# An attention, MoE and bilinear kernel: the order of its first stage as a written-out list, scale constants in four steps, a second key buffer

## The chip, the cores and the metric

The kernel runs on one core of a Trainium2 chip. The metric is the device time of one execution in microseconds (us). The engines are TensorE (PE; PEld is its weight load), VectorE (DVE), ScalarE (ACT), GpSimd (POOL) and SyncE (SP, whose queue issues most DMAs). L with a number is a line of the kernel before.

## The reference

Causal attention with a forget bias, then a mixture of eight experts whose gate is normalised eight times over rows and columns, then a bilinear layer:

```
cum = np.cumsum(np.maximum(s, 0.0), axis=-1)
bias = -(cum[:, :, :, None] - cum[:, :, None, :])
scores = np.where(causal, -1e9, scale * q @ k.T + np.minimum(bias, 0.0))
x = softmax(scores) @ v
P = exp(x @ w_gate - max), eight times divided by row and column sums
out += P[:, e:e + 1] * (np.maximum(x @ w1[e], 0.0) @ w2[e])      for e in 0..7
result = ((out @ w_a) * (out @ w_b)) @ w_out
```

There are 2 batches, 8 heads, 576 tokens each and a head size of 64; the model width is 512, an expert's inner width 1024, the bilinear layer's 1536. All in fp32.

## The kernel before, in words

**Number form.** Most products are made of fp16 pairs: a value is scaled by a power of two and split into a high part (hi, L367 or L372) and a low part, the scaled value less the high one (lo, L382 on VectorE, L376 and L377 on GpSimd). A product is three fp16 matmuls. For each scale the largest value of a tensor is bounded first: by a square with a running sum on ScalarE (`sumsq`, L365, or L602 for the weights), whose squares themselves are not used, or by an absolute maximum on VectorE (`absmax`, L362).

**Attention.** The 1152 tokens are nine tiles of 128; tile 8 holds the two tails of 64. Tiles 0 and 4 open a batch and are done in fp32 (`first_tile`, L1149 to L1220: the maximum L1197, the subtraction L1198, the exponential L1201, transposes L1205 copied by L1208, the product with v L1213, the division L1228 to L1233). The other tiles use the fp16 pairs. For them `k_prep` (L790) makes two forms of each key tile, `kn2` (hi, and beside it the forget bias as three fp16 parts, `caug`) and `kn1` (hi and lo), and `q_prep` (L816) likewise makes `qa` (hi with `qaug`) and `qb`. Each is turned by a DMA transpose on SP's queue, into `ka2` and `ka1` for the keys (L810) and `b` for the queries (L828, L834). Tiles 1 to 3 then take the row maximum (`row_max`, L843, matmuls L856, reductions L860), a shift of it (`shift`, L895) and probabilities (`probs`, L919: exponentials L960 and L972, low parts L974 or L975). Tiles 5 to 8 go by `row_path` (L1012), whose probabilities are turned by DMA transposes (L1039).

**Scale constants.** `scales` (L700) makes for each batch, from the squares of k and q, the scales SK and SQ, the forget bias' scale AL, the product CF and the rest, in a tile `cst` of one column each: `consts` (L728 to L737) and `consts2` (L739 to L755), tiny VectorE instructions. `augs` (L765) makes from AL and CF the forget parts `caug` and `qaug` on GpSimd.

**Expert 0.** As each attention tile comes out (`x_tile`, L1220; its transposes L1244, copies L1249 and L1251, or casts L1254, L1256 with a DMA transpose L1257), expert 0's first product runs for it in quarters (`h_quad`, L1330, matmuls L1343 to L1345) and then its second (`y_part`, L1354, L1363 to L1365). The gate's logits follow (L1292 to L1301). Once all nine tiles are through, experts 1 to 7 run with seven products for eight (`h_seven`, L1736) and then the bilinear layer. Expert 1's weights w1[1] are loaded and split (`w_prep`, L579) before that, in eight pieces of 256 KB.

**What sets the order.** Nothing is issued directly. A `Graph` (L59) records each operation with its engines, a planner's cost and what it reads and writes; `emit` (L235) ranks the operations, moves groups of them by a table `GROUPS`, places them in time by `schedule` (L103), choosing an engine where several are allowed, and issues them in that order. It does so for all operations up to `cut` (attention, expert 0, w1[1]) and then for the rest. An engine runs its instructions strictly in the issued order.

```
        for o in self.ops[:self.cut]:
            o[4] -= o[10]
        self.pool = 1.0
        state = self.schedule(0, self.cut)
```

**Buffers.** `junk` (one tile) takes the squares of k, q and v. `kn1` and `kn2` are one buffer each; `qa` has two, `qb` one.

## Time and profile before

| | |
|---|---|
| median of three runs | 1024.3 us (1023.85 to 1025.38) |
| the profiled execution, first to last instruction | 1023.8 us, 0.5 below the median |
| TensorE busy | 995.2 us, 97% |
| VectorE busy | 777.5 us, 76% |
| ScalarE busy | 547.8 us, 54% |
| GpSimd busy | 103.7 us, 10% |
| chain that ended last | PE 88%, DVE 5%, DMA 4%, ACT, issue and POOL 1% each |

The chain is followed back from the last instruction to what released each step. Shares of the whole hide that the program has two parts: attention with expert 0 up to about 209 us, and dense products after. The windows and timelines below are read for the first part; "idle before" in square brackets names what released an instruction.

### The profile page before, as it was taken

How to read it: one execution, taken by the hardware profiler on the slowest of the kernel's cores; microseconds unless marked ns; L12 is line 12 of the kernel's file. 1: busy time of each engine (PE TensorE's matmuls, PEld its weight loads, DVE VectorE, ACT ScalarE, POOL GpSimd, SP SyncE). 2: the span in 40 equal slices, each digit the busy share in tenths (PEclk: the TensorE clock that was granted, in tenths of full speed). 3: DMA queues.
4: the chain of work that ended last, by engine and by line, in shares of the span. 5: the costliest groups of instructions: out<-in, count | busy, mean ns of one | idle time of the engine just before them, and what ended most of it. 6: DMA issues, size and time to landing. Idle time of an engine off the chain costs nothing.

```text
span 1023.8 us, 18873 instructions
## 1 busy us (share of the span) xinstructions
PE 995.2 (97%) x7514; PEld 630.9 (62%) x7514; DVE 777.5 (76%) x1642; ACT 547.8 (54%) x1029; POOL 103.7 (10%) x163
## 2 busy tenths in 40 slices
PE   6879999999999999999999999999999999999998
PEld 3667776756447646745754774575476464555777
DVE  7789788299957998994899898489988895667402
ACT  7868876375246637734663772565364454545220
POOL 2447616000000000000000000000000000000000
PEclk7689999999999999999999999999999999999999
DMA  9886999222024244114325412422545532313202
GB/s 251 195 144 121 178 161 148 49 83 84 1 89 142 99 179 170 64 47 160 124 83 206 165 42 82 167 82 83 206 165 203 137 83 83 125 42 124 83 25 69
DMA packets 151976, 121.34 MB, mean 119 GB/s; under 512 B 113344, under 2 KB 127680, under 8 KB 147280
## 3 DMA queue, kind: packets, MB, share of 16 engines
...
q8 instruction: 59, 0.97, 0.4%
...
## 4 chain that ended last, share of the span: by engine, by line
PE 88%; DVE 5%; DMA 4%; ACT 1%; issue 1%; POOL 1%; SPq 0%; DVEq 0%; POOLq 0%; ACTq 0%
PE yb L1364 11%; PE yb L1365 11%; PE yb L1363 11%; PE yb L1757 4%; PE yb L1756 4%; PE yb L1755 4%; PE mb L1755 3%; PE mb L1757 3%; PE mb L1756 3%; PE yb L1985 2%; PE yb L1986 2%; PE yb L1987 2%; PE mb L1320 2%; PE mb L1322 2%; PE mb L1321 2%; PE mb L1986 2%
## 5 line engine op out<-in xcount | busy, mean ns | idle before, releaser
L1363 PE MATMUL yb<-wun,ht 128*128 128x512 f16 x504 | 191.0, 379 | 0.0
L1364 PE MATMUL yb<-wun,ht 128*128 128x512 f16 x504 | 191.0, 379 | 0.0
L1365 PE MATMUL yb<-wun,ht 128*128 128x512 f16 x504 | 191.0, 379 | 0.0
L1365 PEld LDWEIGHTS <-ht 128*128 128x128 f16 x504 | 49.3, 98 | 59.4
L1363 PEld LDWEIGHTS <-ht 128*128 128x128 f16 x504 | 49.4, 98 | 58.8
L1364 PEld LDWEIGHTS <-ht 128*128 128x128 f16 x504 | 49.3, 98 | 58.8
L382 DVE SCALAR_TENSOR_TENSOR wun<-stage,sc,wun 128x1024 f16<-128x1024 f32 (+1 forms) x70 | 77.1, 1126 | 8.6 <-ACT wun L368 8.2
L1755 PE MATMUL yb<-sx,wun 128*128 128x288 f16 x288 | 82.4, 286 | 0.0
L1756 PE MATMUL yb<-sx,wun 128*128 128x288 f16 x288 | 82.4, 286 | 0.0
L1757 PE MATMUL yb<-sx,wun 128*128 128x288 f16 x288 | 82.4, 286 | 0.0
L1815 DVE SCALAR_TENSOR_TENSOR acc<-yb,pe,acc 128x512 f32<-128x512 f32 x63 | 47.3, 750 | 41.8 <-PE yb L1365 40.6
L1756 PEld LDWEIGHTS <-wun 128*128 128x128 f16 x672 | 65.7, 98 | 17.8 <-issue 0.7
L1755 PEld LDWEIGHTS <-wun 128*128 128x128 f16 x672 | 65.7, 98 | 17.1
L1757 PEld LDWEIGHTS <-wun 128*128 128x128 f16 x672 | 65.8, 98 | 16.6
L365 ACT ACTIVATE jk<-stage 128x1024 f16<-128x1024 f32 x52 | 54.8, 1054 | 33.6 <-DMA stage<-in_moe_w_dram 33.0
L368 ACT ACTIVATE wun<-stage,sc 128x1024 f16<-128x1024 f32 (+1 forms) x62 | 61.9, 1034 | 19.3 <-PE yb L1365 14.7
L368 ACT ACTIVATE wun<-h,sc 128x1024 f16<-128x1024 f32 x36 | 41.2, 1145 | 27.2 <-issue 23.9
L1755 PE MATMUL mb<-xt,wun 128*128 128x288 f16 x192 | 54.9, 286 | 0.3 <-ACT yb L1774 0.3
L1757 PE MATMUL mb<-xt,wun 128*128 128x288 f16 x192 | 54.9, 286 | 0.0
L1756 PE MATMUL mb<-xt,wun 128*128 128x288 f16 x192 | 54.9, 286 | 0.0
L1344 PE MATMUL mb<-xt,wun 128*128 128x128 f16 x288 | 53.4, 226 | 1.0 <-DVE xt L1251 1.0
L1343 PE MATMUL mb<-xt,wun 128*128 128x128 f16 x288 | 53.5, 226 | 0.3 <-DVE logit L1300 0.3
...
## 6 DMA issues: line engine op xcount, KB each, us to landing
...
```

What stands on the lines that cost most here:

```text
L365: nc.scalar.activation(out, src, AF.Square, accum_out=dst)
L368: nc.scalar.activation(hi, src, AF.Copy, scale=scale)
L382: eng.scalar_tensor_tensor(out=lo, in0=src, scalar=scale, in1=hi, op0=ALU.mult, op1=ALU.subtract)
L1343: nc.tensor.matmul(p, lhsT=wh, rhs=xh, start=(c == 0), stop=False)
L1344: nc.tensor.matmul(p, lhsT=wh, rhs=xl, start=False, stop=False)
L1363: nc.tensor.matmul(pp, lhsT=hh, rhs=wh, start=(f == 0), stop=False)
L1364: nc.tensor.matmul(pp, lhsT=hh, rhs=wl, start=False, stop=False)
L1365: nc.tensor.matmul(pp, lhsT=hl, rhs=wh, start=False, stop=(f == KF - 1))
L1755: nc.tensor.matmul(p, lhsT=wh, rhs=xh, start=first and ch == 0, stop=False, skip_group_check=True)
L1756: nc.tensor.matmul(p, lhsT=wh, rhs=xl, start=False, stop=False, skip_group_check=True)
L1757: nc.tensor.matmul(p, lhsT=wl, rhs=xh, start=False, stop=ch == 1, skip_group_check=True)
L1815: g.add("DVE", 663, lambda t=t, z=z: nc.vector.scalar_tensor_tensor(out=acc[:, t], in0=yb[z], scalar=pe[:, t, e:e + 1], in1=acc[:, t], op0 ...
```

## The change

- The order and the engine choice of every operation up to `cut` are read from a list, `ORDER` (a number is 4 times the operation plus the choice); the ranking, the random seeds and `GROUPS` are gone. The operations after `cut` are placed by the same rules as before.
- Squares of k, q, v and the first tiles' v go to parts of `ka1` and `ka2` that are not yet filled (`spare`), each its own, instead of `junk`.
- The constants are made in four operations: `consts` (SK, SQ), `alpha_` (AL), `factors` (CF), `consts2` (the rest). Forget parts depend on AL or CF alone.
- `caug` may be made on VectorE in four instructions (before: six on GpSimd), `qaug` on either engine.
- `kn2` becomes two buffers `kn[0][0]` and `kn[0][1]` used in turn; `kn1` becomes `kn[1][0]`, still one. The forget half lies first in `kn` and `qa`, so `ut` has 16 columns and needs no memset. `sel` is multiplied only for the first batch's keys.
- `ntail` lies in `xt`, `sc` has 476 columns.

```diff
-        self.stale = True
-        for seed in SEEDS:
-            self.rerank(seed)
-        for o in self.ops[:self.cut]:
-            o[4] -= o[10]
-        self.pool = 1.0
-        state = self.schedule(0, self.cut)
+        state = self.schedule(0, self.cut, None, ORDER)
...
+    def spare(a, i, t):
+        return (ka1, ka2)[a][:, 4 * i:4 * i + 4, t * 128:(t + 1) * 128], ("ka", ("kn1", "kn2")[a], t)
...
-                g.add("ACT", 700, lambda r=r, c=c, t=t, src=src: (
-                    sumsq(mxs[r, c:c + 1], src[t][r], junk[r])),
-                      r=[mk] + (keys[t] if t < 2 * NJ else [keys[t][b]]), w=[mk + (x, j)], rank=rank)
+                jk, jkk = spare(1 - x, 0 if t < 2 * NJ else b, t)
+                g.add("ACT", 700, lambda r=r, c=c, t=t, src=src, jk=jk: (
+                    sumsq(mxs[r, c:c + 1], src[t][r].rearrange("p (a d) -> p a d", a=4), jk[r])),
+                      r=[mk] + (keys[t] if t < 2 * NJ else [keys[t][b]]), w=[mk + (x, j), jkk], rank=rank)
...
-            nc.vector.tensor_scalar(bits(a), bits(a), EXPM, None, op0=ALU.bitwise_and)
-            nc.vector.tensor_scalar(c[:, IK:IK + 2], a, 2.0 ** -6 * h, None, op0=ALU.mult)
-
-        def consts2():
+
+        def alpha_():
             c = cst[:, b]
             col = lambda i: c[:, i:i + 1]
+            a = t4[:, 0:2]
+            nc.vector.tensor_scalar(bits(a), bits(a), EXPM, None, op0=ALU.bitwise_and)
+            nc.vector.tensor_scalar(c[:, IK:IK + 2], a, 2.0 ** -6 * 2.0 ** 63, None, op0=ALU.mult)
             nc.vector.tensor_scalar(col(ESC), col(IK), col(IQ), qk_scale, op0=ALU.mult, op1=ALU.mult)
             nc.vector.tensor_scalar(col(TA), col(ESC), 2.0 ** 17 / qk_scale, bank[:, 130:131], op0=ALU.mult, op1=ALU.add)
             nc.vector.tensor_scalar(bits(col(TB)), bits(col(TA)), EXPM, EXPM, op0=ALU.bitwise_and, op1=ALU.bitwise_xor)
             nc.vector.tensor_scalar(col(AL), col(TB), 2.0 ** 12, None, op0=ALU.mult)
+
+        def factors():
+            c = cst[:, b]
+            col = lambda i: c[:, i:i + 1]
             nc.vector.tensor_scalar(bits(col(TA)), bits(col(TA)), EXPM, None, op0=ALU.bitwise_and)
             nc.vector.tensor_scalar(col(IAL), col(TA), 2.0 ** -13 / qk_scale, None, op0=ALU.mult)
             nc.vector.tensor_scalar(col(CF), col(SK), col(SQ), col(IAL), op0=ALU.mult, op1=ALU.mult)
+
+        def consts2():
+            c = cst[:, b]
+            col = lambda i: c[:, i:i + 1]
             nc.vector.tensor_scalar(col(NAF), col(ESC), col(AL), -1.0, op0=ALU.mult, op1=ALU.mult)
             nc.vector.tensor_scalar(col(APL), col(AL), 14.0 * math.log(2.0), None, op0=ALU.mult)
...
-        g.add("DVE", 930, consts, r=zk, w=[("sk", b)], rank=rank)
-        g.add("DVE", 2050, consts2, r=zk + [("sk", b)], w=[("cst", b)], rank=rank)
+        g.add("DVE", 640, consts, r=zk, w=[("sk", b)], rank=rank)
+        g.add("DVE", 990, alpha_, r=zk + [("sk", b)], w=[("al", b)], rank=rank)
+        g.add("DVE", 490, factors, r=[("al", b)], w=[("cf", b)], rank=rank)
+        g.add("DVE", 950, consts2, r=[("cf", b)], w=[("cst", b)], rank=rank)
...
-            cm = ctmp[:, ts]
+            nc.vector.tensor_scalar(caug[:, ts, :, 0], cumc[:, ts], cc(ci, AL), None, op0=ALU.mult)
+            nc.vector.scalar_tensor_tensor(out=cm, in0=cumc[:, ts], scalar=cc(ci, AL), in1=caug[:, ts, :, 0], op0=ALU.mult, op1=ALU.subtract)
+            nc.vector.tensor_copy(caug[:, ts, :, 1], cm)
+            nc.vector.tensor_tensor(out=caug[:, ts, :, 2], in0=cm, in1=caug[:, ts, :, 1], op=ALU.subtract)
+
+        def fp():
             nc.gpsimd.tensor_scalar(cm, cumc[:, ts], cc(ci, AL), 1.0, op0=ALU.mult, op1=ALU.mult)
             nc.gpsimd.tensor_copy(caug[:, ts, :, 0], cm)
             for x in (1, 2):
                 nc.gpsimd.tensor_tensor(out=cm, in0=cm, in1=caug[:, ts, :, x - 1], op=ALU.subtract)
                 nc.gpsimd.tensor_copy(caug[:, ts, :, x], cm)
...
+        def f2(e):
             o = ones[:, 0:H * 3].rearrange("p (h a) -> p h a", h=H)
-            nc.gpsimd.tensor_scalar(qaug[:, ci], o, cc(ci, CF), 1.0, op0=ALU.mult, op1=ALU.mult)
...
-        ck = [("cst", b) for b in ((ci,) if ci < 2 else (0, 1))]
-        g.add("POOL", 1600, f, r=["cumc"] + ck, w=[("caug", ci)], rank=rank)
-        g.add("POOL", 280, f2, r=["ones"] + ck, w=[("qaug", ci)], rank=rank)
+            e.tensor_scalar(qaug[:, ci], o, cc(ci, CF), 1.0, op0=ALU.mult, op1=ALU.mult)
+
+        ck = [("cst", b) for b in (0, 1)]
+        g.add(("DVE", "POOL"), (561, 1600), (f, fp), r=["cumc"] + ([("al", ci)] if ci < 2 else ck), w=[("caug", ci), "ctmp"], rank=rank)
+        g.add(("POOL", "DVE"), (280, 110), (lambda: f2(nc.gpsimd), lambda: f2(nc.vector)), r=["ones"] + ([("cf", ci)] if ci < 2 else ck), w=[("qaug", ci)], rank=rank)
...
-        hi = lambda: kn2[:, :, 0]
+        z = kc_[0] % NKN
+        kc_[0] += 1
+        hi = lambda: kn[0][z][:, :, 1]
...
-        g.add(("ACT", "POOL"), (713, 690), hi_any(hi, src, cc(ci, SK)), r=krk[t] + kk, w=[("kn2", 0)], rank=rank)
-        g.add(("DVE", "POOL"), (763, 1900), lo_any(lambda: kn1[:, :, 1], src, cc(ci, SK), hi), r=kk + [("kn2", 0)], w=krk[t] + [("kn1", 1)], rank=rank)
...
+        g.add(("ACT", "POOL"), (713, 690), hi_any(hi, src, cc(ci, SK)), r=krk[t] + kk, w=[("kn", z, 1)], rank=rank)
+        g.add(("DVE", "POOL"), (763, 1900), lo_any(lambda: kn[1][0][:, :, 1], src, cc(ci, SK), hi), r=kk + [("kn", z, 1)], w=krk[t] + [("kn", 0, 2)], rank=rank)
...
+        for x, dst, nm in ((0, ka2, "kn2"), (1, ka1, "kn1")):
...
-                g.add("-", 3000, lambda: None, r=[("kn2", 0), ("kn2", 1)], w=behind)
-            g.add("SP", 1600, lambda dst=dst, src_=src_: nc.sync.dma_start_transpose(
-                out=dst[:, :, t * 128:(t + 1) * 128], in_=src_.rearrange("p h a d -> p (h a d)")),
-                r=[(nm, 0), (nm, 1)] + behind, w=[("ka", nm, t)], rank=rank - 5, issue=1300.0)
+                g.add("-", 3000, lambda: None, r=[("kn", z, 0), ("kn", z, 1)], w=behind)
+            g.add("SP", 1600, lambda dst=dst, x=x: nc.sync.dma_start_transpose(
+                out=dst[:, :, t * 128:(t + 1) * 128], in_=kn[x][z * (1 - x)].rearrange("p h a d -> p h (a d)")),
+                r=[("kn", 0, 2 + y) if x else ("kn", z, y) for y in range(2)] + behind, w=[("ka", nm, t)], rank=rank - 5, issue=1300.0)
...
+ORDER = (
+    0, 80, 148, 4, 28, 96, 36, 8, 156, 92, 104, 100, 16, 84, 88, 108, 24, 884, 1632, 12, 76, 888, 20, 160,
+    44, 48, 172, 40, 192, 189, 320, 304, 164, 180, 300, 328, 152, 176, 52, 184, 316, 56, 208, 112, 204, 325, 484, 332,
...
-SEEDS = (0, 0, 0, 0)
+NKN = 2
```

The list moves instructions as follows.

ScalarE at the start, about 17 to 24 us in the profile (p: the two halves of tile 0's probabilities, pt: their transposes, wun: w1[0]'s high parts, acc and raw: k and q). Before:

```order
L1201 ACTIVATE p_0_105<-p_0_105 128x512
L365 ACTIVATE junk,sc<-acc 128x512
L368 ACTIVATE wun_75<-stage_73,sc 128x512 x2
L368 ACTIVATE wun_76<-stage_74,sc 128x512 x2
L1201 ACTIVATE p_1_106<-p_1_106 128x512
L365 ACTIVATE junk,sc<-acc 128x512 x3
L365 ACTIVATE junk,sc<-raw 64x512
L1208 ACTIVATE pt_107<-st_138 128x512
L1208 ACTIVATE pt_108<-st_139 128x512
```
Now:

```order
L1148 ACTIVATE p_0_106<-p_0_106 128x512
L1148 ACTIVATE p_1_107<-p_1_107 128x512
L1155 ACTIVATE pt_108<-st_137 128x512
L294 ACTIVATE wun_75<-stage_73,sc 128x512
L579 DMA vs_95<-in_v_dram 128x8x64
L1155 ACTIVATE pt_109<-st_138 128x512
L291 ACTIVATE ka_93,sc<-acc 128x4x128
L294 ACTIVATE wun_76<-stage_74,sc 128x512 x2
L291 ACTIVATE ka_92,sc<-acc 128x4x128
```
Both exponentials and the first copy of the transposes now stand ahead of all high parts and squares; one high part and a DMA issue stand between the two copies.

VectorE at the first batch's constants (cst; L742 to L745 make AL, L746 to L748 CF, the rest up to L755 what later tiles need; mb and h: expert 0), before, about 43 to 46 us in the profile:

```order
L744 TENSOR_SCALAR cst<-cst 128x1
L745 TENSOR_SCALAR cst<-cst 128x1
L746 TENSOR_SCALAR cst<-cst 128x1
L747 TENSOR_SCALAR cst<-cst 128x1
L748 TENSOR_SCALAR cst<-cst 128x1
L749 TENSOR_SCALAR cst<-cst 128x1
L750 TENSOR_SCALAR cst<-cst 128x1
L751 SCALAR_TENSOR_TENSOR cst<-cst 128x1
L752 TENSOR_SCALAR cst<-cst 128x1
L753 MEMSET cst 128x1
L755 COPY cst<-cst 64x14
L1350 SCALAR_TENSOR_TENSOR h_0_79<-mb_84,h_0_79 128x512
```
Now (L665 to L670 are `alpha_`, L675 to L677 `factors`, L706 opens the forget parts):

```order
L667 TENSOR_SCALAR cst<-cst 128x1
L668 TENSOR_SCALAR cst<-cst,xp_139 128x1
L669 TENSOR_SCALAR cst<-cst 128x1
L670 TENSOR_SCALAR cst<-cst 128x1
L308 SCALAR_TENSOR_TENSOR qb<-acc,cst,qa_100 128x8x64
L675 TENSOR_SCALAR cst<-cst 128x1
L676 TENSOR_SCALAR cst<-cst 128x1
L677 TENSOR_SCALAR cst<-cst 128x1
L308 SCALAR_TENSOR_TENSOR wun_77<-stage_73,sc,wun_77 128x512
L496 TENSOR_REDUCE sc<-xp_140 1x1
L1297 SCALAR_TENSOR_TENSOR h_0_79<-mb_84,h_0_79 128x512
L706 TENSOR_SCALAR caug<-cumc,cst 128x32
```
A low part of q and three other instructions stand between the steps, the six of `consts2` have moved past both row maxima of tile 4 (L1144), and the forget parts, six instructions of GpSimd before, follow here as four (L706 to L709).

GpSimd in the stretch of tiles 1 to 3, about 65 to 85 us in the profile (vs: v's high and low parts; pt: low parts of probabilities). Before:

```order
L975 TENSOR_TENSOR pt_111<-p_0_105,pt_111 128x512
L975 TENSOR_TENSOR pt_107<-p_1_106,pt_107 128x512
L975 TENSOR_TENSOR pt_108<-p_0_105,pt_108 128x512
L514 MEMSET vs_95 128x40x2
L516 MEMSET vs_95 64x4x2 x2
L975 TENSOR_TENSOR pt_109<-p_1_106,pt_109 128x512
L1254 CAST xhl<-xb 128x512
L1256 TENSOR_TENSOR xhl<-xb,xhl 128x512
L372 TENSOR_SCALAR kn_97<-raw,cst 128x8x64
L975 TENSOR_TENSOR pt_110<-p_0_105,pt_110 128x512
```
Now:

```order
L298 TENSOR_SCALAR vs_94<-vs_95,sc 128x8x64
L917 CAST pt_110<-p_1_107 128x512
L298 TENSOR_SCALAR vs_94<-vs_95,sc 128x8x64
L302 TENSOR_SCALAR vs_95<-vs_95,sc 128x512
L303 TENSOR_TENSOR vs_94<-vs_95,vs_94 128x8x64
L921 TENSOR_TENSOR pt_110<-p_1_107,pt_110 128x512
L917 CAST pt_111<-p_0_106 128x512
L921 TENSOR_TENSOR pt_111<-p_0_106,pt_111 128x512
L302 TENSOR_SCALAR vs_95<-vs_95,sc 128x512
L303 TENSOR_TENSOR vs_94<-vs_95,vs_94 128x8x64
```
Two high parts and, of the five low parts of v that VectorE made here before, four (each L302 with L303; the third and fourth follow behind these rows) now stand on GpSimd.

SP's queue: before, every load of q, k and v but three of k stands ahead of the first transpose, which is one of kn. Now six loads of v, three of k and one of q, for the second batch, stand among the first fifteen transposes, and the first two transposes are of qb and qa, the third and fourth of the two kn buffers. The number of transposes is the same, 68. Of the eight loads of w1[1], before six in this queue between transposes near 92 to 103 us and two from ScalarE's queue, two stay between transposes here, four stand at the end around the last transpose of xt, and two are issued from ScalarE's queue.

## Rows read from the trace of the kernel before

**Rows 1.** Windows, two stretches: us, then busy of PE, PEld, DVE, ACT, POOL, clock, DMA share, GB/s.
```profile
63.00:103.00 40.00, 34.73 (x529) 28.59 (x528) 37.52 (x94) 32.82 (x57) 26.50 (x43) 1.00 0.74 130
...
209.00:1024.00 815.00, 810.58 (x5170) 493.92 (x5168) 620.58 (x1235) 398.51 (x733) 16.40 (x31) 1.00 0.32 110
```

**Rows 2.** Windows again, three stretches cut where the granted clock changes.
```profile
12.00:42.70 30.70, 22.22 (x125) 17.22 (x126) 22.26 (x67) 25.76 (x68) 7.99 (x10) 0.50 1.01 236
42.70:56.40 13.70, 11.28 (x100) 7.19 (x98) 11.53 (x39) 11.73 (x30) 8.49 (x17) 1.00 0.78 161
56.40:63.20 6.80, 6.41 (x31) 5.94 (x32) 4.91 (x20) 1.96 (x4) 2.60 (x4) 0.50 0.64 129
```

**Rows 3.** Timeline, VectorE, 15 to 33 us: start, us, engine, line, operation, names, idle before.
```profile
17.13 0.68 DVE L1198 TENSOR_TENSOR p<-ss,mxr 128x512 f32<-128x512 f32 x1
...
27.89 0.69 DVE L362 TENSOR_REDUCE sc<-stage 128x1 f32<-128x512 f32 x1 [1.26 <-DMA stage<-in_moe_w_dram]
```

**Rows 4.** Timeline, ScalarE, 15 to 32 us.
```profile
17.24 2.56 ACT L368 ACTIVATE wun<-stage,sc 128x512 f16<-128x512 f32 x4
19.71 0.61 ACT L1201 ACTIVATE p<-p 128x512 f32<-128x512 f32 x1
20.23 0.61 ACT L365 ACTIVATE junk<-acc 128x512 f16<-128x512 f32 x1
...
22.47 0.63 ACT L365 ACTIVATE junk<-raw 64x512 f16<-64x512 f32 x1
...
23.10 1.06 ACT L1208 ACTIVATE pt<-st 128x512 f32<-128x512 f32 x2
...
30.96 0.63 ACT L602 ACTIVATE wun<-stage 128x512 f16<-128x512 f32 x1 [0.27 <-DMA stage<-in_moe_w_dram]
...
31.59 0.58 ACT L1249 ACTIVATE xt<-st 128x512 f16<-128x512 f32 x1
```

**Rows 5.** Timeline, TensorE, 19 to 34 us and 60 to 63 us.
```profile
23.73 3.68 PE L1213 MATMUL xp<-vf,pt 128*128 128x65 f32 x16 [2.07 <-ACT pt L1208]
...
32.95 0.27 PE L1344 MATMUL mb<-xt,wun 128*128 128x128 f16 x1 [0.40 <-DVE xt L1251]
...
60.88 0.40 PE L856 MATMUL ss<-ka,b 128*128 128x256 f16 x1
```

**Rows 6.** Timeline, VectorE, 33 to 50 us.
```profile
38.95 1.40 DVE L382 SCALAR_TENSOR_TENSOR wun<-stage,sc,wun 128x512 f16<-128x512 f32 x2
...
40.89 0.15 DVE L732 TENSOR_SCALAR sc<-xp 128x2 f32<-128x2 f32 x1
...
41.92 1.05 DVE L382 SCALAR_TENSOR_TENSOR wun<-stage,sc,wun 128x512 f16<-128x512 f32 x1
...
44.90 0.37 DVE L755 COPY cst<-cst 64x14 f32<-64x14 f32 x1
```

**Rows 7.** Timeline, GpSimd (POOL), 33 to 60 us.
```profile
45.58 1.48 POOL L771 TENSOR_SCALAR ctmp<-cumc,cst 128x32 f32<-128x32 f32 x1
...
49.16 0.29 POOL L779 TENSOR_SCALAR qaug<-ones,cst 128x24 f16<-128x24 f32 x1
```

**Rows 8.** Timeline, SyncE queue, 45 to 64 us.
```profile
49.64 1.36 SPq L810 DMA_TRANSPOSE ka<-kn  x1
```

**Rows 9.** Waits, GpSimd 40 to 63 us, ScalarE 50 to 63 us: total, times, longest.
```profile
POOL kn L803 <- DMA ka<-kn: 2.1, 1, 2.1
...
ACT kn L368 <- DVE kn L382: 2.5, 1, 2.5
```

**Rows 10.** Lines, VectorE and GpSimd, 63 to 103 us: count, busy us, mean ns, idle before.
```profile
L382 DVE SCALAR_TENSOR_TENSOR vs<-vs,sc,vs 128x512 f16<-128x512 f32 x5 | 5.5, 1108 | 0.0
...
L377 POOL TENSOR_TENSOR qb<-raw,qa 128x512 f16<-128x512 f32 x1 | 1.5, 1545 | 0.1
```

**Rows 11.** Timeline, SyncE queue, 90 to 106 us.
```profile
99.33 3.86 SPq L594 DMA_DIRECT2D stage<-in_moe_w_dram  x4
```

**Rows 12.** Timeline, ScalarE, 183 to 210 us.
```profile
195.56 0.63 ACT L602 ACTIVATE wun<-stage 128x512 f16<-128x512 f32 x1 [2.96 <-DMA xt<-xhl]
```

More of the change, by code (lines that the diff above doesn't have):

```diff
@@ L90, in add @@
             fn = tuple((lambda q=q: fn0(q)) for fn0 in (fn,) for q in self.queues)
-        self.ops.append([eng, cost, fn, sorted(deps), rank, issue, rel, load, rows, 0.0, *GROUPS.get(self.at, (0.0, 0.0)), self.at])
+        self.ops.append([eng, cost, fn, sorted(deps), rank, issue, rel, load, rows, self.at])
     def begin(self):
@@ L101, in begin, with schedule @@
         self.costs = [o[1] if isinstance(o[1], tuple) else (o[1],) for o in self.ops]
-    def schedule(self, first=0, last=None, state=None):
+    def schedule(self, first=0, last=None, state=None, given=None):
         ops, succ, engs, costs = self.ops, self.succ, self.engs, self.costs
@@ L113, in schedule @@
         order = []
+        for x in given or ():
+            order.append(divmod(x, 4))
+        given, order = order, []
         while pend:
             per = {}
-            for i in pend:
+            for i in [given[len(order)][0]] if given else pend:
                 es, cs, rd = engs[i], costs[i], ready[i]
@@ L119, in schedule @@
                 room = dma - BACKLOG if ops[i][7] else 0.0
-                if len(es) > 1:
+                if given:
+                    k = given[len(order)][1]
+                elif len(es) > 1:
                     pen = PENQ if ops[i][7] else PEN
-                    k = min(range(len(es)), key=lambda k: max(free[es[k]], rd[es[k]], room) + cs[k] + (self.pool * ops[i][11] if es[k] == "POOL" else pen.get(es[k], 0.0)))
+                    k = min(range(len(es)), key=lambda k: max(free[es[k]], rd[es[k]], room) + cs[k] + pen.get(es[k], 0.0))
                 e = es[k]
@@ L297, in forgetting_attention_moe_bilinear_kernel @@
     clampf = clampi.bitcast(F32)
-    sc = const.tile([128, 480], F32, name="sc")
+    sc = const.tile([128, 476], F32, name="sc")
     isx = const.tile([128, NTL], F32, name="isx")
@@ L395, in forgetting_attention_moe_bilinear_kernel @@
     vs = [ap.tile([128, NBLK, H, 130], F16, name=f"vs{b}") for b in range(B)]
-    kn1 = ap.tile([128, H, 2, D], F16, name="kn1")
-    kn2 = ap.tile([128, H, 2, D], F16, name="kn2")
+    kn = [[ap.tile([128, H, 2, D], F16, name=f"kn{x}{i}") for i in range((NKN, 1)[x])] for x in range(2)]
     qa = [ap.tile([128, H, 2, D], F16, name=f"qa{i}") for i in range(2)]
@@ L412, in forgetting_attention_moe_bilinear_kernel @@
     sel = ap.tile([128, H, 2 * H], F32, name="sel")
-    ut = [ap.tile([128, 128], F16, name=f"ut{i}") for i in range(2)]
+    ut = [ap.tile([128, 2 * H], F16, name=f"ut{i}") for i in range(2)]
     cst = ap.tile([128, 3, 16], F32, name="cst")
@@ L423, in forgetting_attention_moe_bilinear_kernel @@
     vf = ap.tile([128, H, 65], F32, name="vf")
-    ntail = ap.tile([H, 128], F32, name="ntail")
     nid = ap.tile([H, H], F32, name="nid")
@@ L508, in forgetting_attention_moe_bilinear_kernel @@
     g.at = "cum"
-    for x, key in ((kn2, ("kn2", 1)), (qa[0], ("qa", 0, 1)), (qa[1], ("qa", 1, 1))):
-        g.add("POOL", 500, lambda x=x: nc.gpsimd.memset(x[:, :, 1], 0.0), w=[key], rank=0.5)
+    for x, key in (*((kn[0][i], ("kn", i, 0)) for i in range(NKN)), (qa[0], ("qa", 0, 0)), (qa[1], ("qa", 1, 0))):
+        g.add("POOL", 500, lambda x=x: nc.gpsimd.memset(x[:, :, 0], 0.0), w=[key], rank=0.5)
     def vone(b):
@@ L528, in forgetting_attention_moe_bilinear_kernel @@
     g.add("POOL", 600, consts_, w=["sel"], rank=0.6)
-    for z in range(2):
-        g.add("POOL", 200, lambda z=z: nc.gpsimd.memset(ut[z], 0.0), w=[("ut", z)], rank=0.7)
     wkey = {}
@@ new lines, in k_prep @@
+        g.add(("DVE", "POOL", "ACT"), (320, 690, 620), (lambda: nc.vector.tensor_copy(kn[1][0][:, :, 0], hi()), lambda: nc.gpsimd.tensor_copy(kn[1][0][:, :, 0], hi()),
+              lambda: nc.scalar.activation(kn[1][0][:, :, 0], hi(), AF.Copy)), r=[("kn", z, 1)], w=[("kn", 0, 3)], rank=rank)
+        if ci != kci[z]:
+            kci[z] = ci
+            if ci < 2 and any(x not in ROWP for x in range(max(ci * NJ, 1), (ci + 1) * NJ) if x not in FIRST):
+                g.add(("POOL", "DVE"), (400, 230), tuple(lambda e=e: e.tensor_scalar(kn[0][z][:, :, 0, 0:2 * H], sel, cc(ci, CF), 1.0, op0=ALU.mult, op1=ALU.mult) for e in (nc.gpsimd, nc.vector)),
+                      r=["sel"] + [("cf", b) for b in bs], w=[("kn", z, 0)], rank=rank)
```

134 lines of the change are left out of this document (28 added, 106 removed), and 65 rows, old and new, of tables (GROUPS, ORDER).

## The prediction

> **What bounds the kernel now.** I read the windows first, because the shares of the whole mix two programs. From 209 us to the end TensorE is busy 810.6 of 815 us at full clock [rows 1]: experts 1 to 7 and the bilinear layer leave 4.4 us of idle time, and the change does not touch their operations. Whatever it does to the time it does before 209 us. There TensorE does 995.2 - 810.6 = 184.6 us of work (table and rows 1), so at most 24 us of idle time are to be had, and some more where the clock is low: the granted clock is 0.50 (1.2 GHz) from 12 to 42.7 us and once more from 56.4 to 63.2 us, and 1.00 (2.4 GHz) between and after [rows 2].
>
> The timelines then say who holds TensorE up. Until 33 us it waits for tile 0, which passes from VectorE to ScalarE and back. From 33 to 61 us it has expert 0 of tile 0 and tile 4's fp32 work, while the constants, the forget parts and the first transposes are made; the first row maximum starts at 60.88 us [rows 5]. From 63 to 103 us VectorE bounds: busy 37.52 of 40 us, TensorE 34.73 [rows 1].
>
> **The change part by part.**
>
> *A, the start.* Tile 0's second subtraction ends at 17.13 + 0.68 = 17.81 [rows 3], but its exponential starts at 19.71, behind four high parts of w1[0] [rows 4]: 1.9 us. Then four squares (first 20.23, last 22.47) stand ahead of the copies of the transposes at 23.10 [rows 4], and the product with v had waited 2.07 us when it started at 23.73 [rows 5]; the first of two copies takes half of 1.06, so 1.5 us were the squares'. That product ends at 27.41; VectorE's division for it comes only behind an absolute maximum that waited 1.26 us for its DMA and ran from 27.89 to 28.58 [rows 3]: 0.9 us allowing 0.25 for the hand-over, an estimate. The copy into xt at 31.59 stands behind a square begun at 30.96 that also waited for its DMA [rows 4]: 0.6 us. All four stand the other way round now: 1.9 + 1.5 + 0.9 + 0.6 = 4.9 us, less one high part of 2.56 / 4 = 0.64 that now stands between the two copies: expert 0 starts about 4.3 us sooner than at 32.95 [rows 5]. I pass on none of it by itself. The row maximum at 60.88 does not wait for expert 0, so TensorE would only stand idle later instead. Bounds: 0 and -4.3.
>
> *B, constants in steps.* Before, the scales are out at 41.5, the last constant ends at 44.90 + 0.37 = 45.27, GpSimd begins the forget parts at 45.58 and ends them and qaug at 49.16 + 0.29 = 49.45, and the first transpose is issued at 49.64 [rows 6, 7, 8]. Now one low part of w2 instead of two stands ahead of L732 (0.70 less, from 1.40 for two [rows 6]); then AL takes six instructions of about 0.2, a low part of q 0.7 to 1.05, CF three of 0.2, a low part of w2 and two others about 1.7, the forget parts on VectorE four of 0.2, and a copy on GpSimd 0.25. From 41.5 - 0.7 = 40.8 that is 1.2 + 0.9 + 0.6 + 1.7 + 0.8 + 0.25 = 5.45 later, 46.3: the first key goes 3.4 us sooner than 49.64, and qb and qa ahead of it. The four instructions are not in the trace as such: the small ones of [rows 6] take 0.15 to 0.37, and I take 0.2. As the loads of the second batch now stand between these transposes in SP's queue, at a pitch of 3.86 / 4 = 0.97 us each [rows 11], part returns: I take -2.5; bounds 0 and -4.5.
>
> *C, the second key buffer.* The forget copy of the next key waited 2.1 us for the transpose of the one before, and the high part 2.5 us for its low part [rows 9]. With two buffers the first wait goes; the second goes where the pair alternates. The lower form kn1 stays single, so its chain of low part, copy and transpose (1.36 us [rows 8]) is next in line. Both waits lie in one stretch: I take -2.5, not their sum; bounds 0 and -3. B and C together bring the row maximum from 60.88 to about 56.
>
> *D, low parts of v.* Five of them cost VectorE 5.5 us in its full stretch, 1.108 us each [rows 10]; four go to GpSimd: -4.4. Against that stand the forget parts of batch 1 and of the tails, eight instructions of 0.2 = +1.6, and two casts' low parts that now are VectorE's. GpSimd takes two instructions for each low part, the longer 1.5 us [rows 10]; eight of at most that are 12.4 us beside 40 - 26.5 = 13.5 us of free time [rows 1]: it just fits. Net -2; bounds -4 and 0.
>
> Row and rule are weighed here. The same low part took 0.70 us beside an idle GpSimd (38.95) and 1.05 beside a working one (41.92) [rows 6], and GpSimd's first forget instruction took 1.48 us at 45.58 [rows 7]. The Trainium skill says in "Advanced Engine Details and Errata", section GPSIMD Details, that GpSimd shares a read and a write interface with VectorE and conflicts with its instructions that read two SBUF inputs, as the low parts do. By that rule the move would give back up to 8 x 0.3 = 2.4 us, an estimate, and D would be about zero. The trace agrees that both slow down. That is D's upper bound as it stands.
>
> *E, squares.* Separate targets may take a wait between squares away; the squares stand beside other work: 0. *F, w1[1].* Four of its loads leave SP's queue at 99.33, 3.86 us [rows 11], for its end; VectorE, not that queue, bounds the stretch [rows 1]: 0, bounds 0 and -0.5, an eighth of those 3.86. *G, the tail.* Expert 1's squares waited at 195.56 for the last of xt [rows 12]. Fewer matmuls of expert 0 are left to cover tile 8's division, cast, transpose and gate, and a load now stands behind that transpose: +1, bounds 0 and +2.
>
> *Clock.* From 56.4 to 63.2 us TensorE works 6.41 us at half clock [rows 2]; a row maximum that comes as expert 0 ends would keep it at 1.00: at best half of it, -3.2. I take -1.5; bounds 0 and -3.2.
>
> *Sum.* -2.5 - 2.5 - 2 - 1.5 + 1 = **-7.5 us**. Against the profiled 1023.8 that is 1016.3; it was 0.5 below the median of 1024.3, so I give **1016.8 us**. All good ends together: -4.5 - 3 - 4 - 3.2 - 0.5 = -15.2, 1009; all bad ones +2, 1026.
>
> **The rivals.**
>
> *1. Swallowed.* VectorE or the single kn1 stays the bound, loads and transposes share SP's queue, and what starts sooner waits later. For it: VectorE's 37.52 of 40 [rows 1], and a DMA share of 0.78 already at 42.7 to 56.4 [rows 2]. Against it: about 24 us of idle TensorE. Then D's lower bound and half of B are left, about -1.5: 1022.8 us.
>
> *2. Slower: TensorE runs dry and falls to half clock.* Expert 0 starts near 28.7 now; if the row maximum stays near 60.88 behind the loads in SP's queue, the work that filled 60.88 - 32.95 = 28 us has to fill 32. If it does not, the granted clock stays at 0.50 in 42.7 to 56.4, where it now is 1.00 over 11.28 us of work [rows 2]. The same work would then take up to twice as long: up to +11.3; as part of it fits into idle time (13.7 - 11.28 = 2.4), I take +11.3 - 2.4 = +9. With half of B and C (-2.5), D (-2) and G (+1) that is +5.5: 1029.8 us. It decides at the clock granted from 43 to 56 us: with no more than half of that stretch at 1.00 the gains are used up (half of 9 against the 4.5 of B, C and D). Against it: the new order spreads expert 0's matmuls more evenly between the fp32 products. The Trainium skill says in "TensorE: Matmul & The Clock Gate", Part 1, that the throttled state is the default and activity releases it. By that rule a thinner start would cost; the trace agrees in so far as 12 to 42.7 us, 22.22 us of work in 30.7, was at 0.50.
>
> *3. More.* A passes on too, because the list keeps TensorE fed from 33 us: the clock rises sooner and the second low stretch goes: -7.5 - 4.3 = about -12: 1012 us and below.
>
> *4. The list is not kept, or the engines' choices differ.* The instruction order shows both as stated; no chance of its own.
>
> **How the numbers follow.** A measurement of this kernel can tell about 0.2%, 2 us, from no change. The forecast, 1013 to 1021, has 0.61, all of it faster. Rival 1 (1021 to 1025) has 0.15: 0.04 faster, 0.10 the same, 0.01 slower. Rival 2 (1025 to 1033) has 0.12, slower. Rival 3 (1006 to 1013) has 0.12, faster. Faster 0.61 + 0.04 + 0.12 = 0.77, same 0.10, slower 0.13. The range from 1008 to 1025 leaves out rival 2 and a third of rival 3, 0.16.
>
> **What would show it.** A: the exponentials in one piece after 17.8 us, expert 0's first matmul near 28.7 instead of 32.95. B: first transpose of kn near 46.3. C: no wait for a kn2 transpose, but some for kn1. B and C: first row maximum near 56 us. D: VectorE's low parts of vs near one in the stretch of tiles 1 to 3, GpSimd without free time there. Clock: 1.00 from 43 us on. Right or wrong as a whole: the dense part begins at about 201.5 instead of 209 us, and takes 815 us as before. A longer dense part, a clock of 0.50 between 43 and 56 us, or a row maximum still near 60 us would make the prediction wrong.

## The result, and the profile after

The new kernel takes **1014.84 us** (median of four runs, 1013.15 to 1018.12) beside 1024.84 for the old one on the same chip; the ratio is 0.991, 95% interval 0.9888 to 0.9933: 7 to 11.5 us faster. The forecast was 1016.8, range 1008 to 1025. The profiled execution is the run of 1013.15 us with a span of 1011.4: in every run about 1.7 us lie around the span. So the profiled execution of before, with its span of 1023.8, was the run of 1025.38 us, the slowest of the three, and not 0.5 us faster than the median as the prediction had it; its sum of -7.5 stands against 1025.4 and gives 1017.9. The two profiled executions are from the slower end of the old kernel's runs and the fastest of the new one's: their spans differ by 12.4 us, the medians by 10.0.

TensorE's and VectorE's totals on the page, and three windows that answer to [rows 2] and [rows 1] (columns as there; from here on L with a number is a line of the kernel whose trace is shown):

```profile
PE 987.7 (98%) x7514; PEld 625.6 (62%) x7514; DVE 777.7 (77%) x1656; ACT 534.8 (53%) x1010; POOL 110.2 (11%) x159
...
42.70:56.40 13.70, 9.84 (x75) 6.67 (x72) 13.22 (x39) 11.22 (x27) 9.99 (x16) 1.00 0.74 124
56.40:63.20 6.80, 6.32 (x79) 4.64 (x78) 6.62 (x20) 5.82 (x11) 6.21 (x8) 1.00 0.92 187
63.00:103.00 40.00, 39.36 (x605) 31.73 (x604) 35.92 (x96) 33.41 (x70) 28.28 (x41) 1.00 0.69 127
```

TensorE's busy time fell from 995.2 to 987.7 us with the same 7514 matmuls. I put these 7.5 us down to the clock: in the dense part TensorE is busy 810.6 us in both, so they were gained ahead of it, where the clock differs. The other 4.9 us of the 12.4 are idle time. From 63 to 103 us TensorE is now busy 39.36 of 40 us (34.73 before), VectorE 35.92 (37.52): the stretch is TensorE's.

The clock column reads 1.00 everywhere, and for the start that is not so. The granted clock is recorded only from its first change on, at 31.64 us here. TensorE's timeline shows what it was before, by the starts of equal matmuls:

```profile
29.44 0.26 PE L1291 MATMUL mb<-xt,wun 128*128 128x128 f16 x1 [0.45 <-DVE xt L1198]
29.50 0.31 PE L1292 MATMUL mb<-xt,wun 128*128 128x128 f16 x1
29.61 0.31 PE L1290 MATMUL mb<-xt,wun 128*128 128x128 f16 x1
...
31.42 0.31 PE L1292 MATMUL mb<-xt,wun 128*128 128x128 f16 x1
31.53 0.28 PE L1290 MATMUL mb<-xt,wun 128*128 128x128 f16 x1
31.64 0.22 PE L1291 MATMUL mb<-xt,wun 128*128 128x128 f16 x1
31.70 0.22 PE L1292 MATMUL mb<-xt,wun 128*128 128x128 f16 x1
```

They stand 0.11 us apart up to 31.53 (1.2 GHz) and 0.055 from 31.64 on (2.4 GHz). Before, the clock rose for good only at 63.2 us, with 13.7 us at full clock from 42.7 [rows 2]. Expert 0's first matmul that waits for VectorE starts at 29.44 instead of 32.95 [rows 5].

The start on ScalarE, the constants and forget parts on VectorE, and SP's queue, as in [rows 4], [rows 6, 7] and [rows 8]:

```profile
16.90 0.63 ACT L1148 ACTIVATE p<-p 128x512 f32<-128x512 f32 x1 [1.80 <-DVE p L1145]
18.22 0.63 ACT L1148 ACTIVATE p<-p 128x512 f32<-128x512 f32 x1 [0.69 <-DVE p L1145]
18.76 0.58 ACT L1155 ACTIVATE pt<-st 128x512 f32<-128x512 f32 x1
...
35.81 0.15 DVE L645 TENSOR_REDUCE sc<-sc 128x2 f32<-128x10 f32 x1
...
38.51 0.17 DVE L659 TENSOR_SCALAR cst<-sc 128x2 f32<-128x2 f32 x1
...
39.74 0.15 DVE L670 TENSOR_SCALAR cst<-cst 128x1 f32<-128x1 f32 x1
...
42.49 0.28 DVE L706 TENSOR_SCALAR caug<-cumc,cst 128x32 f16<-128x32 f32 x1
...
43.32 0.21 DVE L709 TENSOR_TENSOR caug<-ctmp,caug 128x32 f16<-128x32 f32 x1
...
40.62 1.35 SPq L780 DMA_TRANSPOSE b<-qb  x1
42.24 1.24 SPq L774 DMA_TRANSPOSE b<-qa  x1
44.28 4.69 SPq L756 DMA_TRANSPOSE ka<-kn  x3
```

The scales are out at 38.51 (before 41.48, the row behind L732 of [rows 6]), AL at 39.89, the forget parts end at 43.53 (before 49.45), and the first key goes at 44.28 instead of 49.64. Three key transposes take 4.69 us in one piece. The first row maximum, and the wait ahead of it:

```profile
48.84 0.27 PE L802 MATMUL ss<-ka,b 128*128 128x256 f16 x1 [2.06 <-DMA ka<-kn]
...
PE ss L802 <- DMA ka<-kn: 2.1, 1, 2.1
```

48.84 instead of 60.88 us [rows 5]. The last of tiles 1 to 3 starts at 78.9 instead of 91.6, xt's last transpose at 180.56 instead of 192.37, and expert 0's last sum at 196.75 instead of 208.98: the 12 us are all there by 49 to 79 us and stay. From there to the end the two take 814.7 and 814.8 us.

### The profile page after: what moved, and what is told of

Same layout as the page of the kernel before. It is cut to its first block, busy times and chain, and to the rows that moved or that the text cites. A ratio compares the mean times of both kernels' runs of the same rounds, so it can differ in the third digit from the quotient of the medians.

```text
span 1011.4 us, 18813 instructions
## 1 busy us (share of the span) xinstructions
PE 987.7 (98%) x7514; PEld 625.6 (62%) x7514; DVE 777.7 (77%) x1656; ACT 534.8 (53%) x1010; POOL 110.2 (11%) x159
## 4 chain that ended last, share of the span: by engine, by line
PE 92%; DVE 4%; DMA 1%; ACT 1%; SPq 1%; issue 0%; POOL 0%; ACTq 0%; DVEq 0%
PE yb L1312 11%; PE yb L1311 11%; PE yb L1310 11%; PE yb L1704 5%; PE yb L1702 5%; PE yb L1703 5%; PE mb L1702 3%; PE mb L1704 3%; PE mb L1703 3%; PE yb L1934 2%; PE yb L1932 2%; PE yb L1933 2%; PE mb L1267 2%; PE mb L1268 2%; PE mb L1269 2%; PE mb L1932 2%
## 5 line engine op out<-in xcount | busy, mean ns | idle before, releaser
L1712 ACT ACTIVATE ht<-yb 128x288 f16<-128x288 f32 x96 | 38.8, 408 | 31.3 <-PE yb L1704 31.0
L1290 PE MATMUL mb<-xt,wun 128*128 128x128 f16 x288 | 51.5, 222 | 0.6 <-DVE sc L274 0.6
## 6 DMA issues: line engine op xcount, KB each, us to landing
stage<-in_moe_w_dram SPq DMA_DIRECT2D x26, 1024.0 KB, 5.1
md<-wun SPq DMA_DIRECT2D x18, 1024.0 KB, 4.0
wun<-md SPq DMA_DIRECT2D x12, 1024.0 KB, 4.8
stage<-md SPq DMA_DIRECT2D x5, 1024.0 KB, 4.8
```

Of the source, the lines that this page charges most:

```text
L1290: nc.tensor.matmul(p, lhsT=wh, rhs=xh, start=(c == 0), stop=False)
```

## The experiments

**The theories.** *Waits*: the terms of my sum, B -2.5, C -2.5, D -2, each for itself. *Clock*: most of the gain is TensorE's clock, which the new list raises sooner. *Together*: parts and list only work with each other. The first four runs take each by itself, the next four undo one part of the new program, the last four mend two of the first and test what was left. Every time stands beside the old kernel on the same chip (medians 1023.28, 1023.59 and 1023.43 in the three groups); the new kernel was not run again beside them, so small differences to it are read with its interval, 0.9888 to 0.9933, and both by the medians and by the ratios: the old kernel's own median was 1024.84 beside the new one, up to 1.6 us above those three.

Where an order is changed, it is written out for all operations, and the rest keeps its place.

### 1. The clock alone

```diff
+    def fill(n):
+        for x in range(n):
+            nc.tensor.matmul(mb[0][:, 128 * (x % 4):128 * (x % 4 + 1)], lhsT=idb[:, 0:128], rhs=msk[0][:, 0:128], start=True, stop=True)
...
+FILL = {57: 10, 95: 16, 179: 9, 100: 12}
```

> The clock alone: the old program with 47 more 128x128 fp16 matmuls on TensorE (their result is overwritten unread) in its idle places between 15 and 32 us, about 5 us of work at half clock. Nothing else moves. Theory of the clock: full clock from about 33 us, 9 us of busy TensorE at half clock become half as long, of which 2 to 5 us arrive at the end: 1019 to 1022 us. Theory of waits: the row maximum at 60.9 us hangs on the keys, so nothing arrives, or the added work delays tile 0 by up to 1 us: 1024 to 1025 us.

Measured 1025.12 us, ratio 1.0015 (1.0006 to 1.0024). Windows of its trace, cut at the clock's changes:

```profile
24.70:31.60 6.90, 3.87 (x43) 3.50 (x42) 3.12 (x10) 5.07 (x17) 0.00 (x0) 1.00 0.91 232
31.60:45.20 13.60, 12.46 (x101) 11.30 (x102) 10.83 (x47) 12.94 (x33) 7.09 (x9) 0.50 1.18 225
```

The clock rose at 24.75 and fell again at 31.58, just as expert 0 begins, and stayed at half through 13.6 us in which TensorE was busy 12.46. Full clock over those products was what the run was to give, and it did not; what 47 matmuls more did give is 1.5 us of delay, the time that the theory of waits had named. So the clock's worth by itself stays open, and it was not had by filling these idle places.

### 2. The list alone, the parts alone, the start alone

```diff
-        state = self.schedule(0, self.cut)
+        for x in FULL:
+            i, k = divmod(x, 4)
```

> The new order alone: every operation of the old program (one shared square target, constants in two operations, forget parts on GpSimd, one key buffer) in the order and on the engines that the new program has for it; an operation that must wait for the single buffers follows as soon as it can. Theory of waits (my sum: second key buffer -2.5, half of the constants' -2.5 and the forget parts on VectorE): 3.5 us of the gain are lost, about 1018.5 us, first row maximum near 52 us. Theory of the clock (7.5 of the 12.4 us between the two profiled executions are TensorE's own busy time, from a full clock at 31.6 instead of 42.7 us and no second low stretch; the list brings it): about 1015 to 1016 us, with the clock full before 36 us.

> The parts alone: the new program (squares to separate places, constants in four steps, forget parts on VectorE, two key buffers) in the order and on the engines of the old one, the two new steps right behind the one they were cut from. Theory of waits: -3.5 to -5, about 1020 us, first transpose of a key near 46.5 instead of 49.6 us. Theory of the clock: the low clock to 42.7 us stays, at most -1.5: 1023 to 1024 us.

> The start alone: the old program, with ScalarE's and VectorE's instructions up to expert 0's first matmul in the new order (exponentials and copies of the transposes ahead of high parts and squares), all else as before. My sum: expert 0 starts about 4 us sooner, nothing is passed on: 1024 us. Theory of the clock: TensorE reaches full clock some 4 to 10 us sooner than 42.7 us and the products of expert 0 take 0.056 instead of 0.107 us each: -3 to -5, about 1020 us.

Measured 1031.35 (ratio 1.0076, 1.0063 to 1.0088), 1033.79 (1.0102, 1.0087 to 1.0118) and 1033.66 us (1.0105, 1.0091 to 1.0119): all slower than the old kernel, which neither theory had named. They say less than they were made for. In the first two I had resolved conflicts by pulling operations forward: in the second a load of v came to stand ahead of keys in SP's queue and held it from 14.5 to 23.1 us. In the third the squares of weights stood in the new order while their loads came in the old one, and TensorE waited 15.7 us, in three waits, for maxima:

```profile
PE xp L568 <- DVE sc L542: 15.7, 3, 8.2
```

So such a list does not carry over unmended. One thing they do show: in the first the clock was at full from 33.1 us, before the 36 us that the theory of the clock asked for, and the run was 8 us slower all the same. The list alone was mended and run again in 6, the parts alone in 5.

### 3. One key buffer in the new program

```diff
-        z = kc_[0] % NKN
+        zz = kc_[0] % NKN
         kc_[0] += 1
+        z = 0
```

> The new program with one key buffer instead of two (the second one's high parts, forget parts and transposes use the first; eleven operations that must wait for it come later in the order, none sooner). My term C: +2.5 us, 0 to 3, about 1017.3 us. Rival (the order and the buffer hang together: SP's queue then waits for a key that waits for the transpose before it, with queries and loads behind it): +5 us or more, 1020 us. If the buffer is hidden: 1014.8 us.

Measured **1023.98 us**, ratio 1.0008 (0.9997 to 1.0019): without its second key buffer the new program is as slow as the old one. SP's queue, TensorE's waits and two windows:

```profile
44.74 9.31 SPq L761 DMA_TRANSPOSE ka<-kn  x3
54.14 1.28 SPq L779 DMA_TRANSPOSE b<-qa  x1
59.81 2.61 SPq L761 DMA_TRANSPOSE ka<-kn  x2
...
PE ss L807 <- DMA ka<-kn: 7.5, 1, 7.5
...
52.30:62.60 10.30, 7.82 (x37) 6.24 (x38) 7.73 (x24) 7.66 (x19) 4.19 (x6) 0.50 0.55 106
...
52.30:62.60 10.30, 9.14 (x99) 6.56 (x98) 9.82 (x34) 7.71 (x18) 9.79 (x11) 1.00 0.73 146
```

The first key goes at 44.74, as in the new kernel, but the three key transposes take 9.31 us instead of 4.69, the next two begin at 59.81 instead of 50.45, and the row maximum waits 7.5 us instead of 2.1. That is 5.4 us. Then the second price: after a stretch, 38.7 to 52.3 us, in which TensorE works 7.90 of 13.6 us (10.70 in the new kernel) the clock is 0.50 from 52.3 to 62.6 us (the first window; the second is the new kernel's, at 1.00). TensorE's busy time is 993.3 us, 5.6 above the new kernel's 987.7. The two profiled executions have spans of 1022.9 and 1011.4 us: of the 11.5 us between them 5.6 are busy time and 5.9 idle time, nearly all of it this wait. The medians differ by 9.1.

### 4. The other parts undone, one at a time

Constants in one piece, forget parts on GpSimd (VectorE's order, rows of the constants):

```diff
 L670 TENSOR_SCALAR cst<-cst 128x1
-L308 SCALAR_TENSOR_TENSOR qb<-acc,cst,qa_100 128x8x64
 L675 TENSOR_SCALAR cst<-cst 128x1
 ...
+L688 COPY cst<-cst 64x14
+L308 SCALAR_TENSOR_TENSOR qb<-acc,cst,qa_100 128x8x64
 ...
-L706 TENSOR_SCALAR caug<-cumc,cst 128x32
```

> The new program with the constants of a batch made in one piece and the forget parts on GpSimd, six instructions instead of four on VectorE, right behind them. My term B: +2.5 us, 0 to 4.5, about 1017.3 us; first transpose of a key 2 to 3 us later than 44.3, first row maximum as much later than 48.8. Rival (VectorE bounds the stretch, so what leaves it gives time back): 1014 to 1015 us.

Low parts of v on VectorE (four numbers of the list, the choice of engine only; the expectation's seven of ten is a miscount, since only four low parts of v stand on GpSimd in the new kernel):

```diff
-L302 TENSOR_SCALAR vs_95<-vs_95,sc 128x512
-L303 TENSOR_TENSOR vs_94<-vs_95,vs_94 128x8x64
+L308 SCALAR_TENSOR_TENSOR vs_94<-vs_95,sc,vs_94 128x8x64
```

> The new program with all low parts of v on VectorE, as before (seven of ten move back from GpSimd). My term D: +2 us, 0 to 4, about 1016.8 us. Rival (the shared interface: what GpSimd takes over slows VectorE's instructions beside it): 1014 to 1015 us, no difference, since the trace after shows the stretch of tiles 1 to 3 hardly shorter (row maxima 48.8 to 78.9 us, before 60.9 to 91.6).

All squares to one place:

```diff
     def spare(a, i, t):
-        return (ka1, ka2)[a][:, 4 * i:4 * i + 4, t * 128:(t + 1) * 128], ("ka", ("kn1", "kn2")[a], t)
+        return ka1[:, 0:4, 8 * 128:9 * 128], ("ka", ("kn1", "kn2")[a], t)
```

> The new program with all squares of k, q and v written to one place (the last key tile's part of the first key array, filled only later), as before to junk, so that each square waits for the one before it. My term E: 0, 1014.8 us. Rival (ScalarE's 0.13 us of wait at each of 30 squares delays the maxima on which the constants hang, about half of them before 34 us): +2 us, 1016.8 us.

The start as before (ScalarE's order only, and of that three high parts and one square; what VectorE does there stays as in the new kernel):

```diff
 L1148 ACTIVATE p_0_106<-p_0_106 128x512
+L294 ACTIVATE wun_75<-stage_73,sc 128x512
+L294 ACTIVATE wun_76<-stage_74,sc 128x512 x2
 L1148 ACTIVATE p_1_107<-p_1_107 128x512
+L291 ACTIVATE ka_93,sc<-acc 128x4x128
 L1155 ACTIVATE pt_108<-st_137 128x512
```

> The new program with ScalarE's start as before: three high parts of w1[0] ahead of the second exponential and a square ahead of the copies of the transposes; expert 0's first matmul 3 to 4 us later than 29.4. My term A: 0, 1014.8 us. Rival (what TensorE does not do before 48.8 us it must do after, where it is busy without a gap): +2 to +4, about 1018 us.

| undone | median us | ratio to the old kernel | first key's transpose, us |
|---|---|---|---|
| nothing (the new kernel) | 1014.84 | 0.9910 (0.9888 to 0.9933) | 44.28 |
| constants and forget parts (B) | 1016.80 | 0.9938 (0.9923 to 0.9953) | 46.18 |
| low parts of v (D) | 1015.68 | 0.9925 (0.9913 to 0.9937) | 44.60 |
| squares (E) | 1014.80 | 0.9922 (0.9907 to 0.9937) | 44.92 |
| start (A) | 1017.60 | 0.9934 (0.9919 to 0.9949) | 47.31 |
| second key buffer (C) | 1023.98 | 1.0008 (0.9997 to 1.0019) | 44.74 |

By the medians B is worth 2.0 us, A 2.8, C 9.1, D 0.8 and E 0.0; by the ratios 2.9, 2.5, 10.0, 1.5 and 1.2. The intervals of B and A overlap the new kernel's by a little, but the key's transpose says the same, 1.9 and 3.0 us later. By their times D and E can't be told from nothing. B's trace has the row maximum's wait at 4.3 us instead of 2.1:

```profile
PE ss L803 <- DMA ka<-kn: 4.3, 1, 4.3
```

How A arrives is the surprise. Expert 0 starts only 1.2 us later (30.68; 3 to 4 us had been expected), and yet the key is 3.0 us late. VectorE's and TensorE's timelines of that run, and SyncE's queue's waits from 20 to 36 us:

```profile
23.75 0.22 DVE L1176 TENSOR_SCALAR rs<-xp,isx 128x4 f32<-128x4 f32 x1 [2.51 <-PE xp L1161]
...
34.76 0.69 DVE L286 TENSOR_REDUCE sc<-stage 128x1 f32<-128x512 f32 x1 [1.55 <-DMA stage<-in_moe_w_dram]
...
38.42 0.15 DVE L646 TENSOR_REDUCE sc<-sc 128x2 f32<-128x10 f32 x1
...
41.55 0.17 DVE L660 TENSOR_SCALAR cst<-sc 128x2 f32<-128x2 f32 x1
...
35.77 0.37 PE L496 MATMUL xp<-id,sc 128*1 128x128 f32 x1 [2.30 <-DVE sc L470]
...
37.35 0.58 PE L498 MATMUL xp<-sc,ones 1*128 1x1 f32 x2
...
SPq L517 <- DVE wun L309: 3.7, 5, 2.2
```

The same in the new kernel, with 35.81 and 38.51 above:

```profile
33.06 0.69 DVE L285 TENSOR_REDUCE sc<-stage 128x1 f32<-128x512 f32 x1 [0.63 <-DMA stage<-in_moe_w_dram]
...
34.07 0.27 PE L495 MATMUL xp<-id,sc 128*1 128x128 f32 x1 [1.48 <-DVE sc L469]
...
34.94 0.38 PE L497 MATMUL xp<-sc,ones 1*128 1x1 f32 x2
...
SPq L516 <- DVE wun L308: 1.1, 2, 0.7
```

VectorE's division for tile 0 (L1176) waits 2.51 us for the later product, and low parts of weights (L309) stand behind it. SyncE's queue, which loads w2 into the places that these low parts free, waits 3.7 us for them instead of 1.1. So the last maximum of w2 (L286) gets its load late and starts at 34.76 instead of 33.06: 1.7 us. The small products that make scales of the maxima (L496, L498) then have twelve of expert 0's matmuls between them in TensorE's queue, and the clock is 0.50 from 35.5 to 42.4 us in that run: 1.58 us from the one to the other instead of 0.87. The maxima of k and q (L646) come 2.6 us later, the scales 3.0 (41.55). The keys hang on tile 0 by VectorE's queue and, for some 1.3 of the 3 us, by TensorE's queue and clock. This is the one place where a trace here shows the low clock as a cause of delay.

### 5. The parts in the old order

FULL is the old kernel's order here; where an operation's input is now made by another one, the operation is moved back instead of its input forward.

```diff
-        state = self.schedule(0, self.cut, None, ORDER)
-        order = self.order
-        self.schedule(self.cut, None, state)
-        for t, i, k in order + self.order:
+        for x in FULL:
+            i, k = divmod(x, 4)
```

> The parts alone once more, mended: the new program in the old order and on the old engines (forget parts on VectorE), but the three squares that would have pulled a load forward come later instead. If the key buffer's worth lies in the waits of the old trace (2.1 and 2.5 us), with the constants' steps: -3 to -5, about 1019.5 us. If its worth hangs on an order that uses it (SP's queue brings the two key forms of a tile one after the other, so the next copy waits anyway): -1 to +1, about 1023.5 us.

Measured 1025.59 us, ratio 1.0020 (1.0011 to 1.0029), a little worse than either expectation: the parts (B's instructions, C and E; A and D are places and choices in the list) gain nothing in the old order. SP's queue, to be read beside 49.64 of [rows 8], the first row maximum, and last the line of the old kernel that stands ahead of 60.88 of [rows 5]:

```profile
49.09 1.36 SPq L757 DMA_TRANSPOSE ka<-kn  x1
...
53.70 2.71 SPq L757 DMA_TRANSPOSE ka<-kn  x2
...
60.64 3.12 SPq L757 DMA_TRANSPOSE ka<-kn  x2
...
57.83 1.61 PE L1161 MATMUL xp<-vf,pt 128*128 128x65 f32 x13
...
59.69 0.28 PE L803 MATMUL ss<-ka,b 128*128 128x256 f16 x1
...
56.79 3.65 PE L1213 MATMUL xp<-vf,pt 128*128 128x65 f32 x16 [0.49 <-ACT pt L1208]
```

The first key goes 0.55 us sooner, the rest when it went before; and the row maximum stands behind tile 4's fp32 product (L1161) in TensorE's queue, as L856 stood behind L1213 before. Neither row maximum has a wait for a key ahead of it: TensorE comes to it when its place in the queue comes, and what is ready sooner is not asked for sooner.

### 6. The new order without the parts, and the parts without a list

```diff
-        state = self.schedule(0, self.cut, None, ORDER)
+        for seed in SEEDS:
+            self.rerank(seed)
...
+        state = self.schedule(0, self.cut)
```

> The order alone once more, mended: the old program in the new order and on the new engines, where eleven operations that must wait for the single key buffer come later in the order, none sooner. From the run with one key buffer (+9.2 us to the new program) and that with the constants in one piece (+2.0): the sum, about 1026 us; if the two overlap (both delay the same first keys) 1024 us. In both cases the order alone gains nothing against the old kernel's 1023.6.

> All parts of the new program, but the order is made by the old planner from them (old ranking and group offsets, which were chosen for the old program) instead of the written-out list. If the parts carry the gain and any order that knows of the two buffers can use them: 1014 to 1018 us. If the list itself is needed: 1021 us or more.

Measured 1029.74 us, ratio 1.0055 (1.0041 to 1.0069), for the list without the parts, and 1041.41, ratio 1.0170 (1.0154 to 1.0186), for the parts with the old planner (the diff above is the second's). The first is 4 to 6 us slower than its expectation. Its SP queue shows what the list does with one buffer, two windows what the clock did:

```profile
47.14 8.66 SPq L805 DMA_TRANSPOSE ka<-kn  x3
...
61.46 2.61 SPq L805 DMA_TRANSPOSE ka<-kn  x2
...
33.72:50.78 17.06, 11.07 (x108) 7.44 (x108) 12.21 (x43) 9.35 (x20) 7.60 (x15) 1.00 0.73 125
50.78:64.44 13.66, 7.88 (x37) 6.24 (x38) 7.08 (x18) 9.27 (x21) 6.41 (x9) 0.50 0.43 83
```

Three key transposes in 8.66 us and the next two at 61.46, as with one buffer in 3. The list alone costs 6 us, the parts alone 2, both together gain 9 to 10: the theory *together* stands. The list does raise the clock sooner by itself, at 33.7 us instead of 42.7, but the clock falls again at 50.8, while TensorE waits 9.7 us ahead of its first row maximum (56.56), and nothing is gained: the theory *clock* does not stand as it was put. That any order which knows the two buffers can use them is refuted by the planner's 18 us.

## Why the prediction was right, and where it was not

**Direction, time and range** held: -7.5 forecast, -10.0 measured (-7 to -11.5). The path was as said: the first keys sooner, then the row maxima, then everything behind, and a dense part that does not change. The terms did not hold as well as their sum, and that the sum came within 2 us is in part luck: the parts undone one at a time come to 15 to 18 us beside a gain of 10, so they overlap, which the sum did not allow for. One step was wrong under B and C alike: the sum took the keys' waits for TensorE's. [rows 5] has no wait ahead of 60.88, as the row maximum stood behind tile 4's product (5); that it now comes when the keys do is the list's doing, for which the sum had no term.

- *A, 0: wrong, and it is about -2.5 to -2.8, with a part of it undone.* The step that failed is "the row maximum at 60.88 does not wait for expert 0". It does not wait for expert 0's results, but the scales come later when tile 0 does: by the loads that wait for VectorE's low parts behind tile 0's division (1.7 us), and by expert 0's matmuls that stand ahead of the scales' small products in TensorE's queue (1.3 us) (4). I had asked who waits for the moved result and not who stands behind it.
- *B, -2.5: right in size*, -2.0 to -2.9; first key at 44.28, forecast 46.3, because A's 3 us are in it too.
- *C, -2.5: mis-sized, by a factor of nearly 4 in the new order (9 to 10 us) and not there at all in the old one.* The two waits of [rows 9] were the wrong measure. They are what one buffer costs a list that was made around one buffer; the new list issues keys so closely that one buffer would cost it 5.4 us of wait and the clock besides (3).
- *D, -2: open*, -0.8 to -1.5, which the times tell neither from -2 nor from 0. The traces speak for the larger: from the first to the last row maximum of tiles 1 to 3 it takes 30.1 us in the new kernel (48.84 to 78.92), 30.1 with the squares undone (49.46 to 79.58) and 31.6 with D undone (49.21 to 80.85). VectorE is 1.6 us less busy from 63 to 103 us than before; GpSimd spends 7.9 us on the four low parts. The Trainium skill's rule on the shared interface ("Advanced Engine Details and Errata", GPSIMD Details), by which the prediction estimated about zero, is not refuted: the estimate is only the less likely by these traces, and no run here separates the interface from the rest.

```profile
L303 POOL TENSOR_TENSOR vs<-vs,vs 128x512 f16<-128x512 f32 x4 | 5.1, 1280 | 0.3
...
L302 POOL TENSOR_SCALAR vs<-vs,sc 128x512 f32<-128x512 f32 x4 | 2.8, 691 | 0.1
```

- *E, 0: right as far as can be told. G, +1: about right.* From the last row maximum (91.64, 78.92) to the last sum (208.98, 196.75) it takes 117.3 and 117.8 us; expert 1's squares wait 3.75 us instead of 2.96 [rows 12]:

```profile
183.86 0.63 ACT L524 ACTIVATE wun<-stage 128x512 f16<-128x512 f32 x1 [3.75 <-DMA xt<-xhl]
```

- *Clock, -1.5: mis-sized.* In the two profiled executions the same matmuls take 7.5 us less of TensorE, since the second low stretch is gone and the first ends 11 us sooner. How much of that is cause is not settled: 1 could not set the clock, 3 and 6 show it as a result, low after TensorE had starved, and only in 4 (the start) does it delay something. Of the four runs' spread it explains nothing that holds elsewhere: their mean recorded clocks, 1.000, 0.997, 0.996 and 0.985 at 1013.15, 1013.60, 1016.08 and 1018.12 us, stand in the order of the times, but those of the run without B do not (0.988 at 1015.43, 0.991 at 1020.16 us), and such a mean leaves out what lies ahead of the first change.

**The rivals.** *Swallowed* is what the old order does with the same parts (5). *Slower* had the right mechanism in the wrong kernel: the new one does not run dry, since the row maximum now stands ahead of tile 4's product, but with one key buffer it does, and the clock falls there (3), from 52.3 us on; that version comes to 1024.0, not 1029.8. *More*, near 1012, is right in its signs, A passed on, the clock sooner, no second low stretch in the profiled run, but not in its size: the fastest of the four runs took 1013.15 us. *The list is not kept* did not occur.

**Left open**: what the clock would be worth by itself; and whether a second buffer for kn1 as well, for which ScalarE and GpSimd still wait 0.6 and 2.0 us, would bring more. It was not tried. No version that was run can be told to be faster than the new kernel.
